# Attention scores of two heads issued in turn, into two banks that they share with the attention's outputs

## Chip, core and metric

One core of a Trainium2 chip runs the whole kernel. The metric is the time of one execution on the device in microseconds (us). TensorE multiplies matrices and writes to PSUM, which has eight banks; VectorE (DVE in the profile), ScalarE (ACT) and GpSimd (POOL) work on what lies in SBUF, the first two also on PSUM; DMAs are issued from SyncE (SP). Every engine works off its own queue in order, and waits at the head of the queue hold up all that stands behind.

## What is computed

```python
def _attn_ref(q, k, v, f_logit):                  # (4, 8, 768, 48) each
    f = 1.0 / (1.0 + np.exp(-f_logit))
    for t in range(S):
        state = f[:, :, t, :, None] * state + np.einsum('bhd,bhe->bhde', k[:, :, t], v[:, :, t])
        y[:, :, t] = np.einsum('bhd,bhde->bhe', q[:, :, t], state)

x = y as 3072 tokens x 384
x = (max(x @ w_in, 0) ** 2) @ w_out               # 384 -> 2048 -> 384
P = exp(logits of x @ w_gate), eight rounds of row and column normalisation
out = sum over 8 experts of P[:, e] * (max(x @ w1[e], 0) @ w2[e])   # 384 -> 1024 -> 384
```

All of it is in fp32 (the first mixture's weights reach the chip as 64-bit numbers). The state is decayed per channel, so that the attention is computed in chunks.

## The kernel before

**Attention.** The 3072 tokens are 24 chunks of 128, six for each of four sequences. Eight heads of 48 channels lie as four pairs: one head of a pair in partitions 0 to 47, the other in 64 to 111. For each chunk `c` the steps are: a sigmoid of the gates (L312), two scans on VectorE (L319, L325) that make running decays, products of keys and queries with them (L329, L332), the scores (L344), the causal mask on VectorE that also takes them out of PSUM (L349, one instruction for the four pairs of one head), a transpose of the keys (L354, L358), the chunk's contribution to the state (L366) and the state's update (L371, L336), the output (`mix`, L383 from scores and values, L386 from the state), and its way out of PSUM: a rounded part on ScalarE (L417) and the rest on VectorE (L415).

**Scores.** `scores(c, j)` issues the four products of head `j` of each pair, into one bank. For `j` = 0 and 1 these are two steps, `sc0` and `sc1`. From chunk 3 on both use the one buffer of the pool `ps_p`, so `sc1` waits for the mask of `sc0` (`cm0`), and `sc0` of the next chunk for `cm1`; the output `y` has a bank of its own (`ps_y`). In the first three chunks, when the accumulators of the first mixture are still free, `sc1` and every second output use the banks of those.

**First mixture.** Eight blocks of 384 tokens (three chunks each), sixteen steps a block: nine long products (L500) in three roundings, ReLU and square (L505, L508), a split into two roundings (L512 on ScalarE, L516 on VectorE), and nine long products (L526) into three banks of accumulators, two steps later. Block `j` needs the output of its three chunks, the first block that of chunks 0 to 2. Within the first block, step `f` also needs weight block `f`, which is converted from 64-bit numbers: two steps on ScalarE (L909, L912), three on VectorE (L916, L920, L924), a sum on GpSimd (L928), a rounding on ScalarE (L281) and the rest by L284 (on VectorE for ten of the sixteen, on GpSimd for six). The attention of the next block runs between the products of the current one.

**Second mixture.** It follows when the first is done (L679, L730, and VectorE, ScalarE and GpSimd around them); nothing of it is touched.

**What sets the order.** A planner (`Plan`) holds each step with its engine, a cost, a due time and the steps that it needs, and plays them forward; each engine's queue is in the order in which the planner starts the steps. Where TensorE would idle before the first products, it fills in small matmuls (`warm`, L246). So a changed cost, due time or need moves other steps too. Each fp32 product of scores or outputs is carried out as two passes, each with a load of weights and a matmul of its own in the profile; the long products (fp32r) are one pass.

Of the kernel before, what the change touches and what calls it, by code (L numbers as in the profile page):

```python
# [9 lines left out]
F32 = mybir.dt.float32  # L10
# [7 lines left out]
PSUM = bass.MemoryType.PSUM  # L18

B, H, S, DH = 4, 8, 768, 48  # L20
NP = H // 2
# [5 lines left out]
CH = 128  # L27
# [4 lines left out]
CPB = BT // CH  # L32
# [118 lines left out]
def body(tc, fkq, v, wm, wa, wc, gate, seqs, out):  # L151
# [37 lines left out]
    ps1 = ExitStack()  # L189
    ps_acc = ps1.enter_context(tc.tile_pool(name="ps_acc", bufs=1, space=PSUM))  # L190
    ps_p = ps1.enter_context(tc.tile_pool(name="ps_p", bufs=1, space=PSUM))
    ps_y = ps1.enter_context(tc.tile_pool(name="ps_y", bufs=1, space=PSUM))
# [8 lines left out]
    def if_(ok, name):  # L201
        return name if ok else None
# [33 lines left out]
    warm, acc1, tmp = {}, {}, {}  # L236
# [101 lines left out]
    def scores(c, j):  # L338
        kk = kq[c % 3]

        own = c >= CPB or j == 0
        tmp["p", j] = (ps_p if own else ps_acc).tile([128, NP, CH], F32, tag="pp" if own else "a1", name="pp")
        for p in range(NP):
            pe.matmul(tmp["p", j][:, p, :], kk[64 * j:64 * j + DH, 0, p, :], kk[64 * j:64 * j + DH, 1, p, :], start=True, stop=True)  # L344

    def causal(c, j):
        if j == 0:
            Psb[c] = ap2.tile([128, 2, NP, CH], F32, tag="Psb", name="Psb")
        dve.tensor_tensor(out=Psb[c][:, j], in0=tmp["p", j], in1=mask.to_broadcast([128, NP, CH]), op=ALU.mult)  # L349
# [25 lines left out]
    def new_y(c):  # L375
        own = c >= CPB or c % 2 == 0
        tmp["y", c] = (ps_y if own else ps_acc).tile([128, NP, CH], F32, tag="y" if own else "a2", name="y")
# [47 lines left out]
    for c in range(NCH):  # L425
# [5 lines left out]
        b2 = c >= 2  # L431
# [22 lines left out]
        at("sc0", "pe", 0.87, 0, lambda c: scores(c, 0), [("mulk", c), ("mulq", c), if_(c, ("cm0" if c < CPB else "cm1", c - 1))])  # L454
        at("cm0", "dve", 0.6, 0, lambda c: causal(c, 0), [("sc0", c), "masks", if_(b2, ("mix", c - 2))])
        at("sc1", "pe", 0.87, 1, lambda c: scores(c, 1), [("cm0", c)] if c >= CPB else [("sc0", c), if_(c, ("cm1", c - 1))])
        at("cm1", "dve", 0.6, 1, lambda c: causal(c, 1), [("sc1", c), ("cm0", c)])
# [9 lines left out]
        needs = [("cm0", c), ("cm1", c), ("ldv", c), if_(not first, ("sh", c)), if_(c > CPB, ("yl", c - 1)), if_(1 < c <= CPB, ("yl", c - 2 if c < CPB else c - 1))]  # L467
# [123 lines left out]
    def at(us):  # L591
        return n1 + us / 3.0
# [578 lines left out]
```

## Time and profile before

| | us |
|---|---|
| median of 3 runs (2186.46 to 2194.72) | 2186.51 |
| the profiled execution | 2187.32 |
| its span in the profile | 2185.5 |
| TensorE busy (97% of the span) | 2115.9 |
| VectorE busy (61%) | 1328.3 |
| chain that ended last: TensorE | 90% |
| of it L344, the scores | 2% |

The busy time of TensorE counts from the first of overlapping passes to the last. The share over the span is a mean over three stages with different limits: attention and weight conversion up to some 142 us, the first mixture with the rest of the attention up to 550 us, the second mixture after that. The granted clock of TensorE is at half in the first 19 us and full in most of the rest.

### The profile page before, as it was taken

The numbers are of one execution on the slowest core, as the hardware profiler recorded it, in microseconds if no ns is written. First come the engines' busy times: TensorE is split into PE (matmuls) and PEld (weight loads), VectorE is DVE, ScalarE is ACT, GpSimd is POOL, SyncE is SP. The second block draws the span as 40 slices with busy tenths as digits, with TensorE's granted clock in tenths as the row PEclk, the third lists the DMA queues.
The fourth block names the chain that finished last, engine by engine and source line by source line (L and its number), as shares of the span: only waits on it lengthen the run. The fifth ranks groups of instructions, "written<-read, shape, count | busy, mean of one in ns | idle before, by whom it ended". The sixth has DMA issues, their size and how long they took to land.

```text
span 2185.5 us, 27781 instructions
## 1 busy us (share of the span) xinstructions
PE 2115.9 (97%) x10668; PEld 1791.7 (82%) x10668; DVE 1328.3 (61%) x2016; ACT 885.5 (41%) x1505; POOL 648.9 (30%) x642
## 2 busy tenths in 40 slices
PE   8899999999986999999999999999999999999998
PEld 6789899998975888887887888888887888888886
DVE  7974433342365666765767766676668667666764
ACT  4654444443642333432433443344335334433441
POOL 4531100010010433343333333333333243334332
PEclk8899999999987999999999999999999999999999
DMA  6432211110111112111123211121123112111210
GB/s 248 138 115 62 86 57 63 63 56 12 60 55 39 63 55 68 55 64 46 54 68 110 68 54 54 58 68 53 54 68 111 61 54 64 54 61 61 68 44 31
DMA packets 55114, 148.76 MB, mean 68 GB/s; under 512 B 6332, under 2 KB 15548, under 8 KB 54972
## 3 DMA queue, kind: packets, MB, share of 16 engines
q1 hardware_dynamic: 54972, 146.90, 20.4%
q8 instruction: 85, 1.39, 0.3%
q14 instruction: 57, 0.47, 0.1%
HBM read 135.28 MB, written 9.54 MB: 66 GB/s over the span
## 4 chain that ended last, share of the span: by engine, by line
PE 90%; DVE 7%; issue 1%; DMA 1%; POOL 1%; ACT 0%; SPq 0%; POOLq 0%; DVEq 0%; ACTq 0%
PE o L730 34%; PE e L679 32%; PE e L500 9%; PE a L526 8%; PE pp L344 2%; PE y L383 1%; PE y L386 1%; PE lg L541 1%; DVE lo L516 1%; DVE cv_t L916 1%; DVE sg L319 1%; DVE cv_t L924 1%; DVE sg L325 1%; PE ds L366 1%; POOL acc L750 0%
## 5 line engine op out<-in xcount | busy, mean ns | idle before, releaser
L730 PE MATMUL o<-h,w 128*128 128x512 f32 x3456 | 794.4, 390 | 7.7 <-DVE acc L745 7.7
L730 PEld LDWEIGHTS o<-h,w 128*128 128x128 f32 x3456 | 649.5, 188 | 144.5 <-DVE acc L745 8.2
L679 PE MATMUL e<-x,w 128*128 128x512 f32 x3168 | 734.0, 392 | 9.6 <-DVE flag L887 4.5
L679 PEld LDWEIGHTS e<-x,w 128*128 128x128 f32 x3168 | 598.7, 189 | 136.4 <-ACT s L697 5.7
L750 POOL TENSOR_TENSOR acc<-acc,sc 128x512 f32<-128x512 f32 x270 | 349.9, 1303 | 574.7 <-DVE sc L745 566.8
L697 ACT COPY s<-e 128x512 f32<-128x512 f32 x288 | 169.2, 587 | 851.1 <-PE e L679 846.2
L745 DVE TENSOR_TENSOR sc<-o,pb 128x512 f32<-128x512 f32 x270 | 186.3, 690 | 384.9 <-PE o L730 339.5
L719 DVE SCALAR_TENSOR_TENSOR h<-v,h 128x512 fp32r<-128x512 f32 x384 | 277.8, 742 | 1.7 <-ACT h L714 1.3
L714 ACT ACTIVATE h<-v 128x512 fp32r<-128x512 f32 x384 | 242.5, 632 | 41.7 <-DVE v L706 41.6
L651 POOL TENSOR_TENSOR rawa<-rawa 128x256 f32<-128x256 f32 x96 | 84.2, 877 | 552.8 <-DMA rawa<-in_wa_dram 373.8
L706 DVE TENSOR_TENSOR v<-e,s 128x512 f32<-128x512 f32 x288 | 198.2, 688 | 75.5 <-ACT w L664 58.2
L500 PE MATMUL e<-x,w 128*128 128x384 f32 x1152 | 232.5, 346 | 7.6 <-DVE x L415 4.8
L516 DVE TENSOR_TENSOR lo<-g,hi 128x384 fp32r<-128x384 f32 x128 | 83.8, 655 | 234.0 <-ACT hi L512 234.0
L500 PEld LDWEIGHTS e<-x,w 128*128 128x128 f32 x1152 | 201.5, 191 | 16.6 <-DVE x L415 5.0
L526 PE MATMUL a<-hi,w 128*128 128x384 f32 x768 | 199.5, 341 | 0.0
L668 DVE TENSOR_TENSOR w<-rawa,w 128x768 fp32r<-128x768 f32 x192 | 158.1, 824 | 7.5 <-ACT w L664 7.5
L505 ACT ACTIVATE g<-e 128x384 f32<-128x384 f32 x128 | 62.9, 492 | 212.4 <-PE e L500 208.3
L664 ACT CAST w<-rawa 128x768 fp32r<-128x768 f32 x192 | 135.2, 729 | 27.5 <-POOL rawa L653 8.4
L526 PEld LDWEIGHTS a<-hi,w 128*128 128x128 f32 x768 | 140.8, 191 | 0.7 <-issue 0.4
L526 PE MATMUL a<-lo,w 128*128 128x384 f32 x384 | 131.0, 341 | 7.5 <-DVE lo L516 6.6
L329 POOL TENSOR_TENSOR kq<-kq,sg 128x512 f32<-128x512 f32 x24 | 31.8, 1323 | 316.6 <-DMA kq<-in_fkq_dram 167.9
L668 DVE TENSOR_TENSOR w<-rawc,w 128x768 fp32r<-128x768 f32 x96 | 91.6, 954 | 0.3 <-ACT w L664 0.2
(99 smaller groups left out, 1354.4 us busy)
## 6 DMA issues: line engine op xcount, KB each, us to landing
rawa<-in_wa_dram SPq DMA_DIRECT2D x96, 384.0 KB, 3.0
rawc<-in_wc_dram SPq DMA_DIRECT2D x96, 384.0 KB, 3.4
raw<-in_wm_dram SPq DMA_DIRECT2D x16, 768.0 KB, 5.8
pb<-ptd SPq DMA_DIRECT2D x24, 512.0 KB, 3.6
fraw<-in_fkq_dram SPq DMA_DIRECT2D x23, 512.0 KB, 3.8
kq<-in_fkq_dram SPq DMA_DIRECT2D x23, 512.0 KB, 4.9
vt<-in_v_dram SPq DMA_DIRECT2D x24, 192.0 KB, 5.0
x2d<-x2t SPq DMA_DIRECT2D x8, 576.0 KB, 2.8
```

The lines of the kernel that those rows point to most:

```text
L500: pe.matmul(ps, w[:, wl, k * 128:(k + 1) * 128], xx[:, xl, k, :], start=n == 0, stop=n == 3 * KD - 1)
L526: pe.matmul(acc1[j][m], w[:, wl, D + m * 128:D + (m + 1) * 128], g, start=f == 0 and n == 0, stop=f == NF - 1 and n == 2)
L664: act.copy(out=W2[g, k][:, 0, 0:n], in_=src)
L668: dve.tensor_tensor(out=W2[g, k][:, 1, 0:n], in0=src, in1=W2[g, k][:, 0, 0:n].bitcast(F32), op=ALU.subtract)
L679: pe.matmul(ps, w[a], x[b], start=start and n == 0, stop=stop and n == 2, skip_group_check=True)
L697: act.copy(out=snap[g, n], in_=bank[g, "a"])
L706: dve.tensor_tensor(out=vs[g, k], in0=bank[g, k], in1=other, op=ALU.add)
L714: act.activation(out=hs[g // 2, t, f][:, 0], in_=vs[g, k], func=ACTF.Relu)
L719: dve.scalar_tensor_tensor(out=h[:, 1], in0=vs[g, k], scalar=0.0, in1=h[:, 0].bitcast(F32), op0=ALU.max, op1=ALU.subtract)
L730: pe.matmul(ob[q, t, m], w[:, a, c:c + 128], h[:, b], start=f == 0 and n == 0, stop=f == 3 and n == 2)
L745: dve.tensor_tensor(out=dst, in0=ob[q, t, m], in1=pbt[p, e][:, t * TB:(t + 1) * TB], op=ALU.mult)
L750: pool.tensor_tensor(out=acc[p, t, m], in0=acc[p, t, m], in1=sc[q, t, m], op=ALU.add)
```

## The change

The scores of a chunk become one step, `sc`. It takes two buffers of `ps_p`, which now has two, and issues for each pair the product of head 0 and then that of head 1, each into its own bank. Both masks follow. The output of a chunk takes the next buffer of the same pool from chunk 3 on, so `sc` of the next chunk needs both masks (`cm1`) and, from chunk 4 on, the VectorE part of the previous output (`yl`, L415). In the first three chunks the outputs use two of the accumulators' banks in turn. `sc` is entered with a cost of 0.95 (two steps of 0.87 before), and `cm1` is due with `cm0`.

```diff
--- before.py
+++ after.py
@@ -188,8 +188,7 @@
     ap2 = left.enter_context(tc.tile_pool(name="ap2", bufs=2, reuse_waits="tile"))
     ps1 = ExitStack()
     ps_acc = ps1.enter_context(tc.tile_pool(name="ps_acc", bufs=1, space=PSUM))
-    ps_p = ps1.enter_context(tc.tile_pool(name="ps_p", bufs=1, space=PSUM))
-    ps_y = ps1.enter_context(tc.tile_pool(name="ps_y", bufs=1, space=PSUM))
+    ps_p = ps1.enter_context(tc.tile_pool(name="ps_p", bufs=2, space=PSUM))
 
     plan = Plan()
     add = plan.add
@@ -335,13 +334,14 @@
         Sh[c] = ap2.tile([128, NP, 64], F32, tag="Sh", name="Sh")
         dve.tensor_tensor(out=Sh[c], in0=Sst[c % 2], in1=sg[c % 2][:, 0, :, CH:CH + 1].to_broadcast([128, NP, 64]), op=ALU.mult)
 
-    def scores(c, j):
+    def scores(c):
+
         kk = kq[c % 3]
-
-        own = c >= CPB or j == 0
-        tmp["p", j] = (ps_p if own else ps_acc).tile([128, NP, CH], F32, tag="pp" if own else "a1", name="pp")
+        for j in range(2):
+            tmp["p", j] = ps_p.tile([128, NP, CH], F32, tag="pp", name="pp")
         for p in range(NP):
-            pe.matmul(tmp["p", j][:, p, :], kk[64 * j:64 * j + DH, 0, p, :], kk[64 * j:64 * j + DH, 1, p, :], start=True, stop=True)
+            for j in range(2):
+                pe.matmul(tmp["p", j][:, p, :], kk[64 * j:64 * j + DH, 0, p, :], kk[64 * j:64 * j + DH, 1, p, :], start=True, stop=True)
 
     def causal(c, j):
         if j == 0:
@@ -373,8 +373,8 @@
             dve.tensor_copy(out=t[:, :, 0:DH], in_=tmp["m"])
 
     def new_y(c):
-        own = c >= CPB or c % 2 == 0
-        tmp["y", c] = (ps_y if own else ps_acc).tile([128, NP, CH], F32, tag="y" if own else "a2", name="y")
+
+        tmp["y", c] = (ps_p if c >= CPB else ps_acc).tile([128, NP, CH], F32, tag="pp" if c >= CPB else f"a{1 + c % 2}", name="y")
 
     def mix_pair(c, p, rows=64):
         y, vv, kk, st = tmp["y", c], vt[c % 3], kq[c % 3], Sh.get(c)
@@ -451,10 +451,9 @@
             at("mulq", "dve", 0.65, -2, lambda c: mul_q(c, dve), [("scanf", c), ("ldk", c)])
         else:
             at("mulq", "pool", 1.25, -2, mul_q, [("scanf", c), ("ldk", c)])
-        at("sc0", "pe", 0.87, 0, lambda c: scores(c, 0), [("mulk", c), ("mulq", c), if_(c, ("cm0" if c < CPB else "cm1", c - 1))])
-        at("cm0", "dve", 0.6, 0, lambda c: causal(c, 0), [("sc0", c), "masks", if_(b2, ("mix", c - 2))])
-        at("sc1", "pe", 0.87, 1, lambda c: scores(c, 1), [("cm0", c)] if c >= CPB else [("sc0", c), if_(c, ("cm1", c - 1))])
-        at("cm1", "dve", 0.6, 1, lambda c: causal(c, 1), [("sc1", c), ("cm0", c)])
+        at("sc", "pe", 0.95, 0, scores, [("mulk", c), ("mulq", c), if_(c, ("cm1", c - 1)), if_(c > CPB, ("yl", c - 1))])
+        at("cm0", "dve", 0.6, 0, lambda c: causal(c, 0), [("sc", c), "masks", if_(b2, ("mix", c - 2))])
+        at("cm1", "dve", 0.6, 0.1, lambda c: causal(c, 1), [("sc", c), ("cm0", c)])
         misc = ("st", c - 1) if not first else (("st", c - 2) if c else None)
         lg = [("lgc", blk - 2)] if blk >= 2 and q == 0 else []
         if not last:
@@ -464,7 +463,7 @@
             at("st", "dve", 0.35, 2, state, [("ds", c), if_(not first, ("sh", c)), if_(c % NCB >= 2, ("sh", c - 1)), "pads"])
         if not first:
             at("sh", "dve", 0.35, 0, shat, [("st", c - 1), ("scanr", c), if_(c % NCB > 2, ("mix", c - 2))])
-        needs = [("cm0", c), ("cm1", c), ("ldv", c), if_(not first, ("sh", c)), if_(c > CPB, ("yl", c - 1)), if_(1 < c <= CPB, ("yl", c - 2 if c < CPB else c - 1))]
+        needs = [("cm0", c), ("cm1", c), ("ldv", c), if_(not first, ("sh", c)), if_(1 < c < CPB, ("yl", c - 2))]
         if blk:
             at("mix", "pe", 2.1 if not first else 1.1, 2.5, mix, needs)
         else:
```

The work on each engine stays the same, but for the number of filling matmuls (L246 before, L245 after). What the planner makes of it is shown at three places.

TensorE, chunk 13, in the stretch where TensorE is the bound: `pp` are the scores, `e` the first products (L500 before, L499 after), `a` the second ones (L526, L525), `ktr` the transposes. Before:

```order
L344 MATMUL pp<-kq_125 128x128 x4
L500 MATMUL e_2660<-x_2026,w 128x384 x9
L526 MATMUL a_2532<-hi,w 128x384 x2
L526 MATMUL a_2532<-lo,w 128x384
L526 MATMUL a_2533<-hi,w 128x384 x2
L526 MATMUL a_2533<-lo,w 128x384
L526 MATMUL a_2534<-hi,w 128x384 x2
L526 MATMUL a_2534<-lo,w 128x384
L354 MATMUL ktr<-shift,kq_125 128x128 x4
L344 MATMUL pp<-kq_125 128x128 x4
L500 MATMUL e_2703<-x_2026,w 128x384 x9
```

After:

```order
L344 MATMUL pp<-kq_122 128x128 x8
L499 MATMUL e_2664<-x_2012,w 128x384 x9
L525 MATMUL a_2538<-hi,w 128x384 x2
L525 MATMUL a_2538<-lo,w 128x384
L525 MATMUL a_2539<-hi,w 128x384 x2
L525 MATMUL a_2539<-lo,w 128x384
L525 MATMUL a_2540<-hi,w 128x384 x2
L525 MATMUL a_2540<-lo,w 128x384
L354 MATMUL ktr<-shift,kq_122 128x128 x4
L499 MATMUL e_2705<-x_2012,w 128x384 x9
```

The second block of four has gone from behind the transposes, and its products stand in the first block, which has eight.

VectorE, around the last weight conversion of the first block: `cv_t` and `w` are conversion steps, `sg` and `d` the scans, `Psb` the masks, `lo` the rest of the first mixture's hidden values. Before, from the third step on weight 15 to its last:

```order
L924 SCALAR_TENSOR_TENSOR cv_t<-raw_1035,cv_t 128x768
L516 TENSOR_TENSOR lo<-g,hi 128x384
L325 SCALAR_TENSOR_TENSOR sg_128<-sg_128,d_129 128x516
L326 TENSOR_TENSOR minf<-minf,sg_128 128x4
L349 TENSOR_TENSOR Psb<-pp,mask 128x512
L516 TENSOR_TENSOR lo<-g,hi 128x384
L317 MEMSET sg_127 128x8
L318 MEMSET d_129 128x4
L319 SCALAR_TENSOR_TENSOR sg_127<-sg_127,d_129 128x516
L320 TENSOR_SCALAR d_129<-sg_127 128x4
L321 RECIPROCAL d_129<-d_129 128x4
L284 TENSOR_TENSOR w<-cv_t,w 128x768
```

After, the same two ends:

```order
L923 SCALAR_TENSOR_TENSOR cv_t<-raw_1039,cv_t 128x768
L283 TENSOR_TENSOR w<-cv_t,w 128x768
L316 MEMSET sg_125 128x8
L317 MEMSET d_126 128x4
L318 SCALAR_TENSOR_TENSOR sg_125<-sg_125,d_126 128x516
L319 TENSOR_SCALAR d_126<-sg_125 128x4
L320 RECIPROCAL d_126<-d_126 128x4
L349 TENSOR_TENSOR Psb<-pp,mask 128x512
L283 TENSOR_TENSOR w<-cv_t,w 128x768
```

Before, the second scan of chunk 7 (L325), the first scan of chunk 8 (L319) and two `lo` stand between the two ends; after, it is the first scan of chunk 7 (L318) and the rest of weight 14 (L283). One mask stands there in both.

VectorE, ahead of the VectorE part of the output of chunk 2 (`x`), on which the first product of the first mixture waits. Before:

```order
L924 SCALAR_TENSOR_TENSOR cv_t<-raw_199,cv_t 128x768
L317 MEMSET sg_128 128x8
L318 MEMSET d_129 128x4
L319 SCALAR_TENSOR_TENSOR sg_128<-sg_128,d_129 128x516
L320 TENSOR_SCALAR d_129<-sg_128 128x4
L321 RECIPROCAL d_129<-d_129 128x4
L415 TENSOR_TENSOR x_280<-y,x_280 128x3x128
```

After:

```order
L919 TENSOR_SCALAR cv_t<-cv_t 128x768
L923 SCALAR_TENSOR_TENSOR cv_t<-raw_201,cv_t 128x768
L415 TENSOR_TENSOR x_269<-y,x_269 128x3x128
L316 MEMSET sg_125 128x8
L317 MEMSET d_126 128x4
L318 SCALAR_TENSOR_TENSOR sg_125<-sg_125,d_126 128x516
```

The scan of chunk 3 stood ahead of `x` and stands behind it now.

## Rows read from the trace of the kernel before

**Rows 1.** Stretches: length, busy us of PE, PEld, DVE, ACT, POOL; PEclk, DMA, GB/s.
```profile
28.00:142.30 114.30, 95.38 (x590) 79.62 (x590) 112.59 (x132) 67.47 (x105) 65.79 (x36) 0.88 0.45 152
142.30:550.00 407.70, 407.68 (x2859) 369.05 (x2860) 151.13 (x288) 181.71 (x344) 38.78 (x31) 1.00 0.17 57
```

**Rows 2.** TensorE in order of time: start, duration, instruction; the three waits.
```profile
44.52 5.62 PE L500 MATMUL e<-x,w 128*128 128x384 f32 x17 [4.79 <-DVE x L415]
...
130.92 2.00 PE L500 MATMUL e<-x,w 128*128 128x384 f32 x7 [2.43 <-DVE w L284]
...
142.32 3.91 PE L500 MATMUL e<-x,w 128*128 128x384 f32 x21 [0.40 <-DVE w L284]
```

**Rows 3.** TensorE in order of time, around both score blocks of chunk 13.
```profile
302.87 0.34 PE L526 MATMUL a<-lo,w 128*128 128x384 f32 x1
303.14 1.16 PE L344 MATMUL pp<-kq 48*128 48x128 f32 x8
304.23 1.83 PE L500 MATMUL e<-x,w 128*128 128x384 f32 x9
...
307.29 0.34 PE L526 MATMUL a<-lo,w 128*128 128x384 f32 x1
307.46 0.60 PE L354 MATMUL ktr<-shift,kq 128*128 128x128 f32 x4
307.99 1.16 PE L344 MATMUL pp<-kq 48*128 48x128 f32 x8
309.07 1.83 PE L500 MATMUL e<-x,w 128*128 128x384 f32 x9
```

**Rows 4.** The same view, transposes between long products.
```profile
507.73 0.60 PE L354 MATMUL ktr<-shift,kq 128*128 128x128 f32 x4
508.08 0.60 PE L526 MATMUL a<-hi,w 128*128 128x384 f32 x2
```

**Rows 5.** One line's instructions, 142 to 550 us: durations in ns, minimum, median, maximum.
```profile
L344 PEld LDWEIGHTS pp<-kq x272: 182/188/189, 161.9 to 537.7; 48*128 48x128 f32 x136
L344 PE MATMUL pp<-kq x272: 271/272/374, 161.9 to 537.9; 48*128 48x128 f32 x136
...
L386 PEld LDWEIGHTS y<-kq,Sh x240: 129/131/133, 172.0 to 547.1; 48*64 48x64 f32 x120
```

**Rows 6.** Weight loads, then passes, that overlap 113.285 to 113.30 us.
```profile
113.28 0.14 PEld L386 LDWEIGHTS y<-kq,Sh 48*64 48x64 f32 x2 [0.17 <-issue]
...
113.07 0.28 PE L383 MATMUL y<-Psb,vt 128*64 128x128 f32 x2
113.28 0.33 PE L386 MATMUL y<-kq,Sh 48*64 48x128 f32 x2
```

**Rows 7.** End of an output step, its L415, and the next scores.
```profile
315.44 0.43 PE L386 MATMUL y<-kq,Sh 48*64 48x128 f32 x4
...
316.67 0.66 DVE L415 TENSOR_TENSOR x<-y,x 128x512 fp32r<-128x512 f32 x1
...
319.13 1.16 PE L344 MATMUL pp<-kq 48*128 48x128 f32 x8
```

**Rows 8.** VectorE in order of time, ahead of its last weight conversion.
```profile
133.65 0.55 DVE L516 TENSOR_TENSOR lo<-g,hi 128x384 fp32r<-128x384 f32 x1
134.12 2.87 DVE L325 TENSOR_TENSOR_SCAN sg<-sg,d 128x516 f32<-128x516 f32 x1
...
137.57 1.16 DVE L516 TENSOR_TENSOR lo<-g,hi 128x384 fp32r<-128x384 f32 x1
138.69 0.07 DVE L317 MEMSET sg<- 128x8 f32 x1
...
140.38 1.89 DVE L284 TENSOR_TENSOR w<-cv_t,w 128x768 fp32r<-128x768 f32 x1
```

**Rows 9.** VectorE in order of time, ahead of L415 of chunk 2.
```profile
39.52 2.64 DVE L319 TENSOR_TENSOR_SCAN sg<-sg,d 128x516 f32<-128x516 f32 x1
...
43.94 0.53 DVE L415 TENSOR_TENSOR x<-y,x 128x384 fp32r<-128x384 f32 x1
```

## The prediction

> **What bounds the kernel now.** I read the busy times by stretch first, because the shares over the span mix three stages [rows 1]. From 28 to 142.3 us VectorE is busy 112.59 of 114.30 us and TensorE only 95.38: here the conversion of the sixteen first-layer weight blocks, done on VectorE between the scans and masks of the attention, sets the pace. From 142.3 to 550 us TensorE is busy 407.68 of 407.70 us: it never waits. After 550 us the second mixture runs, which the edit doesn't touch and which moves as a whole. Next the waits of TensorE in order of time [rows 2]. In the first 142 us it waits 4.79 us for the first block's x (L415) and 2.43 and 0.40 us for converted weights (L284); the last of these waits is at 142.32, inside the product that uses weight block 15. So the time is: when the last weight is converted, and then the sum of all TensorE work that stands behind it in the queue. A microsecond that TensorE saves behind 142.3 counts in full. One that it saves earlier only makes it wait longer for VectorE.
>
> **What a block of scores costs.** Today the four products of one head are one block; all lie in the same half of the array's rows and one bank. In fp32 each product is two passes, so a block is 8 rows. In the chunk shown [rows 3] the last product ahead of it starts at 302.87, the block at 303.14 and the product behind it at 304.23. That is 1.36 us from neighbour to neighbour, where two neighbours without a block between them stand 0.17 apart (307.29 to 307.46). A block thus costs 1.18 us (with the third decimal kept). Where the transposes (L354) stand right ahead of it, the two together take 307.29 to 309.07 = 1.78, less 0.17 = 1.61; transposes alone, beside long products, cost 0.35 [rows 4]; the block then costs 1.26. Inside a block one pass takes 272 ns from start to end [rows 5], and the block 1.16 us: the last pass starts 0.88 behind the first, the first is 0.10 longer than the rest (373 or 374), so passes follow each other every (0.88 - 0.10) / 7 = 0.112 us.
>
> Behind 142.3 us stand 34 such blocks (272 rows of 8 each [rows 5]), for 17 chunks: 25 at 1.18 and 9, behind transposes, at 1.26, together 40.8 us.
>
> **What the change makes of them.** Now the two heads alternate: 16 passes, one head in array rows 0 to 47 and the other in 64 to 111, each into its own bank. The trace of before has no block with that pattern, so I bound it. The nearest row is the last step of the attention, L386, whose two heads also alternate between array rows 0 to 47 and 64 to 111 (and, other than the scores, between column halves as well). There both heads' passes run at the same time [rows 6]: two loads of 0.13 us [rows 5] end within 0.14, two passes of 128 columns within 0.33, where in turn the second would end 0.112 later. If the scores do the same, eight pairs take what eight passes take now: a block of 16 passes costs 0.27 (into the block) + 0.88 + 0.01 (the pair's offset) + 0.20 (out of it) - 0.17 = 1.19 us. Then 17 x 1.19 = 20.2, and TensorE saves 40.8 - 20.2 = **20.6 us** behind the last weight. If the two halves take turns, the block is 0.27 + (0.10 + 15 x 0.112) + 0.20 - 0.17 = 2.08 us, 17 x 2.08 = 35.4, and only 5.4 us are saved, one way into and out of a block less for each chunk. I take the first end, because L386 is the one row with both array halves in turn.
>
> The Trainium skill, page "TensorEngine Tiling (Array Packing)", Key Properties, says that different tiles can load and multiply at the same time; that goes further than L386 shows, which has both row and column halves apart. The page "TensorE: Matmul & The Clock Gate" gives 3.07 times, not 4, for four row tiles (Measured speedup vs the span model). By that share of the ideal, as an estimate, a pair would take 0.112 / 0.77 = 0.146 us in place of 0.112, 7 x 0.034 x 17 = 4.0 us more in all; no run here shows it, and the sum below does not use it.
>
> **What moves across the last weight.** In TensorE's queue the product that waits for weight 15 has 15 second products (L526 groups) ahead of it before and 14 now, so one more stands behind it: nine passes at 0.17, +1.6 us. The numbers of transposes, state and output steps behind it are unchanged, and all 17 chunks of scores stay behind it.
>
> **When the last weight is converted.** VectorE has no slack there, so I count what stands ahead of the last L284 in its queue. One scan group less (L319 with its small neighbours: 138.69 to 140.38, 1.7 us), one second scan less (L325: 2.87 us at 134.12), one L516 less (0.55 to 1.16 us) [rows 8]; all other groups (48 conversion steps, 13 masks, 6 L415, 5 states) are as many as before. That is 5.1 to 5.7 us less work. Against it stands the start of the kernel, where VectorE now has both masks of a chunk in one go and may wait for TensorE where before it had a scan to do; the whole idle time between 28 and 142.3 is 1.7 us now and can grow. I take -4.5 us, with ends -8 and +1. In this stretch L415 of chunk 2 moves ahead of the scan of chunk 3 (39.52 to 43.94 [rows 9]), so the first long product should start 4 us earlier. That counts for nothing by itself, since the weights set the end of the stretch. TensorE can follow: it has 7 x 1.18 + 1.6 = 9.9 us less to do before weight 15, and was 0.4 us early there [rows 2].
>
> **The added wait.** The scores of a chunk now need the previous chunk's L415, because its output lies in one of the two banks. While they wait, the whole of TensorE's queue stands behind them. Cover: the output step ends at 315.44 + 0.43 = 315.87, L415 ends at 316.67 + 0.66 = 317.33, so 1.5 us later; the next scores start at 319.13 [rows 7], 3.3 us behind the output step, and the new order puts the state step or one more long product into that gap as well. So at least 1.8 us are to spare, and I cost the wait at nothing. The old wait of the second head for the first head's mask goes; it cost nothing behind 142.3 either.
>
> **The sum.** The profiled run took 2187.3 us for a span of 2185.5. 2187.3 - 20.6 + 1.6 - 4.5 = 2163.8. The median of the runs shown is 0.8 below the profiled one, so **2163 us**, -1.1%.
>
> **The rivals.**
> *Turns.* The two array halves take turns, because 128 columns of weights are loaded for each pass (a load every 0.11 us, as long as the pass) and the loads share a path. For: in a block of today loads and passes are equally close. Against: the paired loads of L386. Sum: -5.4 + 1.6, and -3 for the weights, since the three early blocks get no shorter: 2187.3 - 6.8 - 0.8 = 2179.7, so 2177 to 2182. The Trainium skill speaks for this one: the page "TensorE: Matmul & The Clock Gate" (Step-by-step: what each phase is for) has one read port for all weight loads; the paired loads of L386 show that this alone doesn't put them in a row.
>
> *Turns with a drain, slower than before.* Each change between array halves might cost what a change of tile form costs: from the last L383 pair at 113.07 to L386 at 113.28 it is 0.21, against 0.112 in step, 0.10 more [rows 6]. In 16 passes there are 7 changes (if a product keeps its two passes together) to 15. On top of the turns that is 17 x 0.7 = 12 to 17 x 1.5 = 25 us: 2192 to 2205. It decides against the change from about 0.03 us for each of 15 changes. Against: L386 changes halves inside a pair without any such gap.
>
> *The wait bites.* Overlap holds, but L415 is queued behind a scan and both masks of the next work on VectorE: 1.7 + 1.2 + 1.4 = 4.3 us against 1.8 to 2.3 to spare, so at most 2.5 us in each of the 11 chunks that follow another closely, 27 us; or VectorE loses its gain at the start. The queue has masks behind L415, not ahead, at most of these places, so some 8 us: 2171, within 2167 to 2180.
>
> **How the numbers follow.** Forecast 0.72, by itself 2158 to 2170 (weights -8 to +1, a pair up to 0.118 in place of 0.112, 0.8 us). Wait or lost weights 0.08, turns 0.14, drain 0.06. The range reaches over the turns: **2158 to 2182**; left out are the drain and the tails. A measurement of this kernel tells about 0.5% (11 us) from no change, so faster means under 2175.6 and slower over 2197.4: the forecast and most of the wait give 0.78 faster, the turns and the lower end of the drain 0.17 the same, the rest 0.05 slower.
>
> **What would show it.** In the changed kernel's profile a block of scores has 16 rows in about 1.17 us (right), in about 2.05 (turns), or more (drain). TensorE has no wait from the last L284 to the end of the attention; a wait of scores on L415 there would show the third rival. The last weight wait stands near 138 in place of 142.3, and the first L500 near 39 to 41 in place of 44.5. The stretch from the last weight wait to the end of the attention shortens by 19 us, and nothing changes after it. I am wrong if the block's 16 passes are not paired, or if the weights come later than 143.

## The result, and the profile after

| | before, us | after, us |
|---|---|---|
| median of the runs beside each other | 2186.57 | 2158.41 |
| the same comparison made again | 2185.74 | 2160.32 |
| the profiled execution (first comparison) | 2187.32 | 2158.78 |
| its span | 2185.5 | 2157.1 |
| TensorE busy | 2115.9 | 2083.4 |
| VectorE busy | 1328.3 | 1323.9 |

By the medians the change makes the kernel faster by 28.2 us in the first comparison and by 25.4 us in the second. The ratios of the two kernels, which are not quite the quotients of the medians, are 0.986 (95% interval 0.9836 to 0.9884) and 0.9881 (0.9865 to 0.9898). The forecast was 23.5 us less, 2163 us in a range from 2158 to 2182; the first median lies at the lower edge of that range, and one of its runs (2155.79) below it. The direction and the main term are right; one term is too small.

In the changed kernel the scores are L344 still, the first products L499, the second ones L525, the last step of a weight's conversion L283, `lo` L515 and the mask L349. First TensorE in order of time around chunk 13's scores, which answers to [rows 3]: start, duration, instruction.

```profile
305.83 1.16 PE L344 MATMUL pp<-kq 48*128 48x128 f32 x16
306.93 0.62 PE L525 MATMUL a<-hi,w 128*128 128x384 f32 x2
```

Sixteen passes now stand in 1.16 us, where [rows 3] has eight. The product ahead of them starts at 305.56, so from neighbour to neighbour it is 1.36 us, as for one old block. All 17 blocks behind the weights measure so; first to last start is 0.890 us in each.

The stretches of the profiled execution, which answer to [rows 1] (length, busy us of PE, PEld, DVE, ACT, POOL; PEclk, DMA, GB/s):

```profile
28.00:134.21 106.21, 83.59 (x559) 69.25 (x558) 104.05 (x121) 66.25 (x103) 58.09 (x32) 0.90 0.49 163
134.21:536.00 401.79, 401.49 (x2945) 368.57 (x2946) 156.42 (x301) 189.77 (x357) 43.88 (x36) 1.00 0.18 58
```

The picture is the one of before: VectorE full up to the last weight, TensorE full behind it. The boundary has moved from 142.3 to 134.2. The whole idle time of TensorE behind it is 0.30 us, one wait for `lo` at 141.02, and no wait of scores is left there.

The waits of TensorE that answer to [rows 2], and the one wait of scores on the output ahead of them (L415):

```profile
37.37 1.67 PE L499 MATMUL e<-x,w 128*128 128x384 f32 x8 [1.52 <-DVE d L317]
...
73.51 0.49 PE L344 MATMUL pp<-kq 48*128 48x128 f32 x2
74.51 1.16 PE L344 MATMUL pp<-kq 48*128 48x128 f32 x14 [0.52 <-DVE x L415]
...
82.60 1.65 PE L499 MATMUL e<-x,w 128*128 128x384 f32 x4 [4.45 <-DVE w L283]
...
129.27 1.49 PE L499 MATMUL e<-x,w 128*128 128x384 f32 x7 [0.79 <-DVE d L317]
131.85 0.61 PE L499 MATMUL e<-x,w 128*128 128x384 f32 x2 [1.09 <-ACT w L280]
134.21 3.04 PE L499 MATMUL e<-x,w 128*128 128x384 f32 x16 [1.74 <-DVE w L283]
```

The last weight wait comes 8.1 us earlier than in [rows 2]. Two of these rows are put down to a MEMSET on VectorE (`d`, L317) that follows the true releaser at once: at 37.37 that is `x` (L415), at 129.27 the last step of weight 14. The wait at 74.51 is the price of the shared banks; 8 us later TensorE waits 4.45 us for a weight, so nothing of it is paid.

Where the 28.5 us between the two profiled executions lie, by three places that are easy to find in both (the last weight wait; the first wait of the second mixture, at 636.19 before and 608.72 after; the end):

| stretch | before | after | less |
|---|---|---|---|
| start to the last weight wait | 142.32 | 134.21 | 8.1 |
| from there to the first wait of the second mixture | 493.9 | 474.5 | 19.4 |
| the rest, with what lies outside the span | 1551.1 | 1550.1 | 1.1 |

The second row was forecast at 19.0 and is right. The first was forecast at 4.5, so it is 3.6 us off. So the experiments ask two things: is it really the pairing of the array's halves that makes the 19.4, and where do the 3.6 us more at the start come from?

### The profile page after: what moved, and what is told of

The parts are those of the page before. It is cut to its first block, busy times and chain, and to the rows that moved or that the text cites. A ratio compares the mean times of both kernels' runs of the same rounds, so it can differ in the third digit from the quotient of the medians.

```text
span 2157.1 us, 27848 instructions
## 1 busy us (share of the span) xinstructions
PE 2083.4 (97%) x10686; PEld 1765.9 (82%) x10686; DVE 1323.9 (61%) x2016; ACT 886.1 (41%) x1505; POOL 646.8 (30%) x642
## 4 chain that ended last, share of the span: by engine, by line
PE 89%; DVE 6%; DMA 1%; issue 1%; POOL 1%; ACT 1%; SPq 0%; POOLq 0%; DVEq 0%; ACTq 0%
PE o L729 35%; PE e L678 33%; PE a L525 8%; PE e L499 8%; PE y L383 1%; PE y L386 1%; PE pp L344 1%; DVE cv_t L923 1%; PE lg L540 1%; DVE cv_t L915 1%; DVE lo L515 1%; DVE sg L318 1%; DVE cv_t L919 0%; POOL acc L749 0%; PE ds L366 0%
## 5 line engine op out<-in xcount | busy, mean ns | idle before, releaser
L499 PE MATMUL e<-x,w 128*128 128x384 f32 x1152 | 228.0, 341 | 10.9 <-DVE w L283 7.4
L499 PEld LDWEIGHTS e<-x,w 128*128 128x128 f32 x1152 | 199.8, 189 | 17.7 <-DVE w L283 8.8
L515 DVE TENSOR_TENSOR lo<-g,hi 128x384 fp32r<-128x384 f32 x128 | 85.0, 666 | 206.3 <-ACT hi L511 206.3
L525 PE MATMUL a<-hi,w 128*128 128x384 f32 x768 | 199.5, 341 | 0.0
L525 PE MATMUL a<-lo,w 128*128 128x384 f32 x384 | 131.0, 341 | 11.0 <-DVE lo L515 10.9
L525 PEld LDWEIGHTS a<-hi,w 128*128 128x128 f32 x768 | 139.9, 191 | 1.5 <-issue 0.3
```

The costliest lines, as they stand in the source:

```text
L499: pe.matmul(ps, w[:, wl, k * 128:(k + 1) * 128], xx[:, xl, k, :], start=n == 0, stop=n == 3 * KD - 1)
L525: pe.matmul(acc1[j][m], w[:, wl, D + m * 128:D + (m + 1) * 128], g, start=f == 0 and n == 0, stop=f == NF - 1 and n == 2)
```

## The experiments

**The heads in turn.** In the experiments "in turn" means the four products of head 0 and then the four of head 1, in place of the alternation that the change makes. The joint step and the two shared banks stay; only the order of the eight products changes. (Code is shortened where it has `...`.)

```diff
-        for p in range(NP):
-            for j in range(2):
-                pe.matmul(tmp["p", j][:, p, :], ...)
+        for j, p in [(j, p) for j in range(2) for p in range(NP)]:
+            pe.matmul(tmp["p", j][:, p, :], ...)
```

> The changed kernel with one edit: in the joint step of scores the four products of head 0 come first and then the four of head 1 (same banks, same waits, same order of all other work). Theory A, alternation lets the two array halves work at once: without it the 16 passes take 0.10 + 15 x 0.112 = 1.78 us from first to last start in place of 0.89, so 17 x 0.89 = 15 us more behind the last weight, and 0 to 2 us more ahead of it: 2173 to 2176 against 2158.8. Theory B, the gain came from one joint block with one way in and out and from the new order of the queues, or the chip pairs the halves anyway: within 3 us of the changed kernel.

Measured: 2173.59 us (2170.24 to 2179.07), ratio 0.9936 (0.9914 to 0.9958). TensorE around chunk 13's scores:

```profile
301.54 1.71 PE L343 MATMUL pp<-kq 48*128 48x128 f32 x16
303.18 1.15 PE L498 MATMUL e<-x,w 128*128 128x384 f32 x5
```

The block is 1.71 us long where the changed kernel has 1.16. From the last weight wait to the end the kernel takes 8.9 us more, and 17 x (1.71 - 1.16) is 9.4: so the alternation alone is worth about 9 us there. That is less than the 15 us of theory A; that the median falls into A's range is luck, since in the profiled execution another 7.8 us lie ahead of the weights (the last weight wait is at 142.05, with the clock at half from 8.4 to 29.0 us). Yet the block is shorter than sixteen passes in a row would be (0.10 + 15 x 0.112 = 1.78 from first to last start; measured 1.438). In the single records the second head's first pass starts at 509.30, while three passes of the first head are still to start (509.40 to 509.63). Some passes found a partner across the border of the two heads: without that, 17 blocks would be longer by another 17 x (1.78 - 1.44) = 5.8 us, an estimate from the same rows. So pairing is about 15 of the 19.4 us, and most of the rest is the one way in and out of a joint block, as the prediction had it for turns (5.4 - 1.6). How far past the border a pass can reach is what the next run asks.

**The heads by twos.** Two products of head 0, two of head 1, and again.

```diff
-        for p in range(NP):
-            for j in range(2):
+        for j, p in [(j, p) for h in range(2) for j in range(2) for p in (2 * h, 2 * h + 1)]:
```

> The heads alternate every two products (two of head 0, two of head 1, again) instead of every one. With the heads wholly in turn (the first experiment), eight passes of one head and then eight of the other took 1.438 us from first to last start, not the 1.78 of sixteen passes in a row: the first pass of the second head started while about three passes of the first head were still to come. Theory of a reach of some three passes: with four passes of a head in a row nearly every pass finds a partner, and a block takes 0.9 to 1.05 us from first to last start (0.890 in the changed kernel); behind the weights at most 17 x 0.15 = 2.6 us more than the changed kernel. Rival, only neighbours in the queue pair: 3 pairs at the changes of head and ten single passes, about 1.4 us and 17 x 0.5 = 9 us more behind the weights.

Measured: 2157.56 us in one run. The block:

```profile
304.46 1.26 PE L343 MATMUL pp<-kq 48*128 48x128 f32 x16
305.65 0.62 PE L524 MATMUL a<-hi,w 128*128 128x384 f32 x2
```

First to last start is 0.991 us in all 17, one step of 0.10 more than with strict alternation, and far from the 1.4 of the rival. The work of the other half needn't be the next instruction; with four passes in a row nearly all pair. (The single run's time is as low as the changed kernel's, though from the last weight wait to the first product of the second mixture it takes 2.1 us more, 455.5 against 453.4. Its last weight wait comes 2.2 us earlier, and its clock at the start was full; see the last section.)

**The first seven chunks in turn.** All that stands behind the weights is the changed kernel's; only the early blocks are long again.

```diff
-        for p in range(NP):
-            for j in range(2):
+        for j, p in [(j, p) for j in range(2) for p in range(NP)] if c < 7 else [(j, p) for p in range(NP) for j in range(2)]:
```

> The changed kernel; only chunks 0 to 6, whose scores stand ahead of the last converted weight, have their heads one after the other. Theory A, the conversions on VectorE set that stretch: the last weight wait stays at 134.2 within 1 us, and the time within 1 us of 2158.8. Theory B, the shorter early blocks are where the unforeseen 3.6 us ahead of the last weight came from: the wait moves back by 2 to 4 us, and so does the time, 2161 to 2163.

Measured: 2161.49 us (2159.94 to 2163.55), ratio 0.9872 (0.9832 to 0.9912). By the times alone that is hardly apart from the changed kernel; the trace is clearer, because both executions had the same clock in the first 28 us (0.88). VectorE's waits in order of time from 18 to 33 us, first of the kernel before, then of the changed one, then of this one:

```profile
19.88 0.69 DVE L349 TENSOR_TENSOR Psb<-pp,mask 128x512 f32<-128x512 f32 x1 [3.79 <-PE pp L344]
27.97 0.69 DVE L349 TENSOR_TENSOR Psb<-pp,mask 128x512 f32<-128x512 f32 x1 [0.78 <-PE pp L344]
```

```profile
19.39 0.69 DVE L349 TENSOR_TENSOR Psb<-pp,mask 128x512 f32<-128x512 f32 x1 [1.11 <-PE pp L344]
27.37 0.56 DVE L415 TENSOR_TENSOR x<-y,x 128x384 fp32r<-128x384 f32 x1 [1.02 <-ACT x L417]
29.94 0.35 DVE L371 TENSOR_TENSOR S<-Sh,ds 128x192 f32<-128x192 f32 x1 [0.72 <-PE ds L366]
```

```profile
21.07 0.69 DVE L348 TENSOR_TENSOR Psb<-pp,mask 128x512 f32<-128x512 f32 x1 [1.35 <-PE pp L343]
29.60 0.56 DVE L414 TENSOR_TENSOR x<-y,x 128x384 fp32r<-128x384 f32 x1 [1.57 <-ACT x L416]
32.72 0.35 DVE L370 TENSOR_TENSOR S<-Sh,ds 128x192 f32<-128x192 f32 x1 [1.26 <-PE ds L365]
```

VectorE, which sets the pace, waits for TensorE in the first 33 us: for scores, and for the output and the state that stand behind them. With the early blocks in turn each of these places comes 1.7 to 2.8 us later, the first long product at 40.15 in place of 37.37, and the last weight wait at 137.22 in place of 134.21. What is lost at the start is still there 100 us later, and 2.8 of the 3.0 us are there already at the first long product, so they are the loss of the first three blocks. (The first of them loses most: the clock is at half from 9.8 to 16.6 us in both executions, when the short block is nearly done and the long one has just begun, so it takes 3.06 us in place of 1.23.) Of these 3 us, 0.9 may be chance: the very first scores start at 9.75 in place of 8.88, ahead of anything that was edited, and the start of two kernels that are alike up to there differs by 1.5 us (first long product at 37.01 in the last experiment below, 38.55 in the one with two scans ahead). So the early blocks are worth 2 to 3 us, and theory B holds.

**The first three chunks in turn.** The same line with `c < 3`.

> The changed kernel, with the heads in turn in the scores of chunks 0 to 2 alone. With chunks 0 to 6 in turn all waits of TensorE from the first product of the first mixture on came 2.8 to 3.0 us later. Theory of the start: before the first mixture TensorE is on the path, and its first three score blocks carry that: 3 x 0.55 us at full clock, up to twice that at half clock, so the first long product and all behind it 1.6 to 3 us later, 2160 to 2161.5. Rival, chunks 3 to 6 carry it: the last weight wait stays at 134.2 and the time at 2158.4.

Measured: 2165.25 us (2162.25 to 2169.72), ratio 0.9881 (0.9826 to 0.9936). The last weight wait of the profiled execution is at 141.36. By itself this decides nothing, since the clock was at half from 8 to 28 us, so that two of the three blocks took 3.1 us each. But the run with all heads in turn had nearly the same clock there (0.65 against 0.64). Its first long product comes at 44.56, here at 44.54; its last weight wait at 142.05, here at 141.36. So chunks 3 to 6, in turn only there, cost 0.7 us, and the rival, that they carry the loss, falls. The size of the loss can't be read from this trace. Its lower two runs, 2162.25 and 2162.89, are 2 to 4.5 us above the changed kernel.

**The first product late.** Is it the first long product that carries the loss, or VectorE's queue ahead of it? Here TensorE alone is held up, and VectorE's order stays.

```diff
+        for _ in range(42 if i == 0 else 0):
+            pe.matmul(warm["t"], ident, ident, start=True, stop=True)
```

> The changed kernel, with 42 more filling matmuls on TensorE ahead of the very first product of the first mixture (42 x 0.107 = 4.5 us, of which 1.5 fill the wait there, so that product ends 2.7 to 3 us later). VectorE's order is as in the changed kernel. Theory A, VectorE is what passes a delay on: it has no wait for TensorE between 30 and 54 us, and TensorE waits 8.5 us for it at 54.4, so the last weight wait stays at 96.9 us behind where the first product stood (134.2 in a run with the same clock at the start) and the time at 2156 to 2159. Theory B, the first long product itself is on the path, since in four kernels of these experiments the last weight wait follows it by 96.8 to 97.1 us wherever it stands: last weight wait 2.7 us later, 2160.5 to 2161.5.

> The changed kernel once more, on the same chip as the experiment with the late first product, so that the two are read side by side: 2156 to 2159, with the last weight wait 96.9 us behind the first long series of products.

Measured: 2160.65 us (2157.1 to 2165.13) with the late product, 2160.32 (2157.25 to 2161.71) for the changed kernel beside it. TensorE of the late one:

```profile
36.55 9.54 PE L497 MATMUL warm<-shift 128*128 128x128 f32 x84
45.85 1.83 PE L501 MATMUL e<-x,w 128*128 128x384 f32 x9
...
56.79 0.44 PE L527 MATMUL a<-lo,w 128*128 128x384 f32 x1 [2.71 <-DVE lo L517]
...
136.62 1.65 PE L501 MATMUL e<-x,w 128*128 128x384 f32 x4 [1.74 <-DVE w L283]
```

The expectation counted 42 passes; each fp32 product is two, so it was 84 and 9.5 us. The test is the harder for it: the long series stands 8.4 us later (45.85 against 37.44 in the changed kernel beside it), but TensorE's wait for `lo` shrinks from 8.49 to 2.71 us. The last weight wait is 2.26 us later (136.62 against 134.36). Of that, 0.97 was there already at 30 us, ahead of the edit; the other 1.3 come by way of ScalarE, for which VectorE waits 2.70 us at 50.75. So a late first product costs 1.3 of 8.4 us. The times tell nothing: both kernels are within 0.4 us of each other, and the changed kernel itself is above the 2156 to 2159 that was expected. By the trace theory A holds in substance, though it expected none, and the fixed distance of 96.9 us between the two places, on which B rested, is an effect of VectorE's queue and no law.

**Two scans later, in the kernel before.** Two of VectorE's scans (the second of chunk 7 and the first of chunk 8) are kept behind the last weight conversion, as the change has them.

```diff
-        at("scanr", ..., [("sigr" if c < CPB else "sig", c), if_(c, ("scanf", c - 1)), "scan0"])
-        at("scanf", ..., [("scanr", c), ("sig", c)])
+        at("scanr", ..., [("sigr" if c < CPB else "sig", c), if_(c, ("scanf", c - 1)), "scan0", if_(c >= 8, ("cvl", NF - 1))])
+        at("scanf", ..., [("scanr", c), ("sig", c), if_(c >= 7, ("cvl", NF - 1))])
```

> The kernel before; only the planner's needs are extended so that the second scan of chunk 7 and the first of chunk 8 come behind the last weight conversion in VectorE's queue, as in the changed kernel. TensorE's queue is the same as before. Theory A, as in the prediction, VectorE's work ahead of the last L284 sets the stretch: the wait moves from 142.3 to about 137.7 (1.7 + 2.9 us less), the time to 2182.7. Theory B, TensorE itself is the bound from the wait for weight 14 (130.92) on, since it was only 0.40 us early for weight 15: the wait vanishes, and 0.4 us is all that is gained, 2186.9.

Measured: 2187.44 us (2184.71 to 2196.23), ratio 1.0005 (0.9985 to 1.0025). No gain. TensorE shows why, with VectorE's last step of weight 15 and the stretch between weights 14 and 15 (length, busy us, PEclk as the third number from the end):

```profile
141.33 1.50 PE L500 MATMUL e<-x,w 128*128 128x384 f32 x7 [2.27 <-DVE w L284]
142.76 2.07 PE L344 MATMUL pp<-kq 48*128 48x128 f32 x8
...
150.26 1.16 PE L344 MATMUL pp<-kq 48*128 48x128 f32 x8
151.35 4.95 PE L500 MATMUL e<-x,w 128*128 128x384 f32 x27
```

```profile
147.22 0.96 DVE L284 TENSOR_TENSOR w<-cv_t,w 128x768 fp32r<-128x768 f32 x1 [0.48 <-ACT w L281]
```

```profile
142.60:149.60 7.00, 7.00 (x25) 6.62 (x24) 6.19 (x11) 2.36 (x4) 2.82 (x4) 0.51 0.30 102
```

The wait for weight 15 is gone, but the product of weight 15 starts 10 us after that of weight 14 all the same: two score blocks and two second products stand between them. (All times of this execution are some 10 us late, since its clock was at half up to 54 us.) But TensorE is that slow there because its clock, behind the wait for weight 14, is at half for 7 us: the first score block takes 2.07 us, the second 1.16. The weight itself is ready at 148.18, 3.2 us before TensorE comes to it. At full clock that stretch would be 3.5 us shorter, an estimate from the row, and TensorE would come to weight 15 when it is ready. The kernel before has the same fall of the clock at the same place, from 131.8 to 138.6 us, and waited only 0.40 us for weight 15 [rows 2]. So there, with the clock at half, TensorE was as much the limit as VectorE, and theory B holds. What the scans would give with a full clock between weights 14 and 15, which the changed kernel has, this run doesn't show.

**The same two scans ahead again, in the changed kernel.**

```diff
-        add(("cvl", n), ..., [("cvh", n)])
+        add(("cvl", n), ..., [("cvh", n)] + ([("scanf", 7), ("scanr", 8)] if n == NF - 1 else []))
```

> The changed kernel, with the second scan of chunk 7 and the first scan of chunk 8 put back ahead of VectorE's last weight conversion (where the kernel before has them); one output step of TensorE moves between the products of weights 14 and 15 by that. Theory A, VectorE's queue sets the last weight also in the changed kernel: the last weight wait moves from 134.2 by 2.87 + 1.7 = 4.6 us, to about 138.8, and the time to 2162 to 2164. Theory B, TensorE itself sets the pace there, as it did when the same two scans were moved the other way in the kernel before: the wait grows, but less than 2 us of it reach the end, 2158 to 2160.5.

Measured: 2162.2 us (2159.79 to 2163.83), ratio 0.9866 (0.9813 to 0.9919). TensorE:

```profile
134.35 0.43 PE L383 MATMUL y<-Psb,vt 128*64 128x128 f32 x2 [2.30 <-DVE Psb L349]
...
140.62 2.71 PE L499 MATMUL e<-x,w 128*128 128x384 f32 x14 [0.92 <-DVE w L283]
```

The last weight wait is 6.3 us later than in the changed kernel's second execution (134.36). At the first long product it is 1.1 late already (38.55 against 37.44), so 5.2 are the scans' and what they moved, close to the 4.6 expected. But an output step of 2.9 us now stands ahead of that wait, so at the first product of the second mixture only 2.3 us are left (591.05 against 588.76), and 1.2 without the late start. The median, 2 to 4 us above the changed kernel's, looks like theory A; the trace is nearer to B. The scans cost 1 to 4 us, and the run leaves open how much.

**All scans from chunk 6 on later, in the changed kernel.** As the kernel-before variant above, with `c >= 6` in both lines.

> The changed kernel; only the planner's needs are extended so that all scans of chunks 6 and later come behind the last weight conversion, which takes about 7 us of VectorE's work from ahead of it and moves the scores of chunk 6 behind it. Theory A, VectorE sets the stretch: TensorE's waits of 1.2, 1.3, 0.8, 1.1 and 1.7 us between 119 and 134.2 shrink, the last weight wait ends 3 to 6 us earlier, and with 1.2 us of scores moved behind it the time is 2154 to 2157. Theory B, TensorE's own work sets it: within 1 us of 2158.8.

Measured: 2159.47 us (2158.2 to 2162.41), ratio 0.9866 (0.9826 to 0.9906). The time is that of the changed kernel. In the trace the weight-15 product comes 2.6 us earlier (131.57), though the first long product is 1.3 us later. Of what that gains, 1.2 us are paid behind the weight, where the scores of chunk 6 now stand, and up to 1.7 us go to the clock, which is at half there from 132.6 to 136.0 us. The first product of the second mixture starts at 587.29 us, in the two executions of the changed kernel at 587.62 and 588.76. So work that is put off past the last weight is paid behind it where it is TensorE's. Whether putting off scans alone gains a microsecond or two is less than these runs can tell.

**The output step in two halves.** [Rows 6] had shown that a change of tile form costs 0.10 us more than a step in form. The output step changes seven times in each chunk; here its four pairs from the scores come first, then the four from the state.

```diff
-        for p in range(NP):
-            mix_pair(c, p)
+        for p in range(NP):
+            for j in range(2):
+                pe.matmul(y[...], vv[...], Psb[c][:, j, p, :], start=p == 0, ...)
+        if st is not None:
+            for p in range(NP):
+                for j in range(2):
+                    pe.matmul(y[...], st[...], kk[...], start=False, ...)
```

> The changed kernel, with the output step written so that the four pairs from scores and values (L383) come first and the four pairs from the state (L386) behind them, instead of in turn. Each change of the tile's form costs about 0.10 us more than a step of the same form by the trace (0.21 against 0.11); six of eight changes of a chunk go, and 15 such output steps stand behind the last weight. Theory: TensorE saves 6 x 0.1 to 0.14 in each, 9 to 13 us in all, 2146 to 2150. Rival, the changes cost nothing, since the row halves run on their own: 2158.4.

Measured: 2146.67 us (2146.16 to 2147.09), ratio 0.9797 (0.9745 to 0.9849): 12 to 14 us below the changed kernel, and the fastest of all. An output step of the changed kernel, then of this one:

```profile
316.19 0.44 PE L383 MATMUL y<-Psb,vt 128*64 128x128 f32 x4
316.56 0.43 PE L386 MATMUL y<-kq,Sh 48*64 48x128 f32 x4
...
318.76 0.43 PE L386 MATMUL y<-kq,Sh 48*64 48x128 f32 x4
319.13 1.83 PE L499 MATMUL e<-x,w 128*128 128x384 f32 x9
```

```profile
311.50 1.09 PE L394 MATMUL y<-Psb,vt 128*64 128x128 f32 x16
312.52 1.09 PE L398 MATMUL y<-kq,Sh 48*64 48x128 f32 x16
313.54 1.83 PE L506 MATMUL e<-x,w 128*128 128x384 f32 x9
```

From the first pass to the next product it was 2.94 us and is 2.04: 0.15 us for each of the six changes, more than the 0.10 of [rows 6]. Fifteen such steps stand behind the last weight, 15 x 0.90 = 13.4 with the third decimal kept. From the last weight wait to the first product of the second mixture the kernel takes 441.0 us, the changed kernel's second execution 454.4 (588.76 - 134.36): 13.4 less. (In both of these the clock is at half for 3.4 us right behind the weights. In the first execution of the changed kernel it is not, and there it takes 453.4 us.)

## Where the prediction was right, and the step that failed

**What bounds the kernel: right.** Behind the last weight TensorE is busy 401.49 of 401.79 us, and what it saves there is saved in full. (Ahead of it the prediction names three waits of TensorE, 7.6 us together, of 18.9 us idle between 28 and 142.3 us [rows 1]. The others are waits for `lo` and for masks. The sum doesn't rest on them.)

**The score block: right to the hundredth.** Forecast 1.19 us, measured 1.36 - 0.17 = 1.19, and the stretch behind the weights shortens by 19.4 us against 20.6 - 1.6 = 19.0. The bound from L386 was the right one, although it was an inference from one row that differs in column halves too. Turns and turns with a drain are out: they needed a block of 2.05 us or more. Even with the heads wholly in turn the block is 1.71. Two halves side by side lose 0.01 us in a block (0.890 against 0.88 from first to last start). The Trainium skill, page "TensorE: Matmul & The Clock Gate" (Measured speedup vs the span model), gives 3.07 times in place of 4 for four row tiles; by that share the prediction estimated 4.0 us lost. For two halves this trace doesn't agree; four tiles were not run here.

**The added wait: right, with one place more.** Scores never wait for L415 behind the weights. They do once before, 0.52 us at 74.51 (1.29 us at 74.67 in the second execution), and nothing of it is passed on: the weight wait behind it ends 8.1 us later in both, at 82.60 and 82.77. "No wait from the last L284" is off by the 0.30 us for `lo`.

**When the last weight is converted: the step that failed.** The term was -4.5 us, with ends -8 and +1, and measured -8.1. It was worked out as 5.1 to 5.7 us less work in VectorE's queue, against which about 1 us was set for a worse start. VectorE's own rows divide what was measured. They show the time up to the last weight wait in the kernel before, in the changed one and in the one with seven chunks in turn (length, busy us of PE, PEld, DVE):

```profile
0.00:142.30 142.30, 119.22 (x744) 99.50 (x744) 130.08 (x168) 77.28 (x121) 72.94 (x54) 0.87 0.52 183
```

```profile
0.00:134.21 134.21, 107.56 (x753) 88.13 (x753) 123.51 (x160) 77.10 (x121) 67.46 (x50) 0.90 0.56 194
```

```profile
0.00:137.22 137.22, 111.02 (x754) 92.97 (x754) 123.60 (x160) 77.16 (x121) 67.27 (x50) 0.89 0.56 190
```

Its work is 6.6 us less (130.08 to 123.51), about 1 us more than forecast. Its idle time, the length less that, is 12.2, then 10.7 and 13.6 us: 1.5 us less where 1 us more was forecast. So some 2.5 of the 3.6 us are idle time, and the start did not get worse but better: in the first 28 us VectorE is idle 10.5 us before and 8.5 us after (28.00 less the 17.49 and 19.46 of the last section). With the same clock and the same work, the run with seven chunks in turn has nearly all of the 3.0 us of its later weight (2.9) as idle time of VectorE.

The view on which "VectorE has no slack" rested begins at 28 us [rows 1], and 10.5 of the 12.2 us idle lie ahead of that. There VectorE waits for TensorE: up to 33 us, 3.79 + 0.78 = 4.6 us in the kernel before, 1.11 + 1.02 + 0.72 = 2.9 in the changed one, and 1.35 + 1.57 + 1.26 = 4.2 when the early blocks are long again. The sentence that failed is "One that it saves earlier only makes it wait longer for VectorE". It is true of the first long product (8.4 us late cost 1.3), and so is "That counts for nothing by itself". It is false of the scores ahead of it, for which VectorE itself waits: with seven early blocks in turn, at the same granted clock, the last weight came 3.0 us later, of which 2 to 3 are theirs.

**What is not settled.** The kernel before was profiled with a slower clock in the first 28 us than the changed one (0.82 against 0.88). Half speed for 3.4 us more, (0.88 - 0.82) x 2 x 28, is up to 1.7 us of the 8.1, so the 1.5 us less of idle time between these two executions may be clock in part. The two comparisons of medians (28.2 and 25.4 us) leave the gain beyond the forecast between 2 and 5 us. Why VectorE's work shrank by 1 us more than the steps that were counted is not shown. What the scans are worth alone is open too: put off in the kernel before they gave nothing (ratio 1.0005), with TensorE at half clock as the limit, and put back in the changed one they cost 1 to 4 us.

## What to carry to other kernels

Where small fp32 products use half of the array's rows, issue those of the two halves mixed, into two banks: two blocks then take the time of one, and the passes needn't even alternate strictly. Beside that, group passes of one tile form: here six changes fewer in a step were worth as much as half of the whole change. And before writing that an early saving "is only waited away", look into the first microseconds as well: what matters is whether the engine that sets the pace itself waits for the saving engine anywhere. Its busy and idle time from the very start to the place where the next engine takes over show that at once.

## What the runs showed of the hardware

**The two row halves reach past each other.** With eight passes of one half and then eight of the other, first to last start is 1.438 us, not 1.78; by fours it is 0.991; in strict alternation 0.890. In the single records of the first of these, a pass of the idle half can start while some three passes of the busy half that stand ahead of it are still to start.

**The clock at the start is not the same in each execution.** The first 28 us of the kernel before, of the run by twos, of the changed kernel and of the run with three chunks in turn (length, busy us, PEclk as the third number from the end):

```profile
0.00:28.00 28.00, 23.84 (x155) 19.88 (x156) 17.49 (x37) 9.82 (x17) 7.15 (x18) 0.82 0.84 310
```

```profile
0.00:28.00 28.00, 23.86 (x226) 18.86 (x226) 21.01 (x43) 12.37 (x20) 9.41 (x19) 1.00 0.92 336
```

```profile
0.00:28.00 28.00, 23.97 (x195) 18.87 (x196) 19.46 (x40) 10.86 (x18) 9.37 (x19) 0.88 0.85 312
```

```profile
0.00:28.00 28.00, 22.94 (x134) 19.40 (x135) 15.29 (x34) 8.46 (x14) 6.40 (x18) 0.64 0.83 310
```

In the run by twos TensorE is at 2.4 GHz in all of these 28 us; in the last one it is at 1.2 GHz from 8 to 28 us, and has got through 134 passes in place of 226. In these three kernels, which differ little up to there, the last weight wait stands at 131.97, 134.21 and 141.36 us. The spread is larger than the effects looked for at the start, so a few microseconds there can be read only from executions with the same clock in these rows. What decides it wasn't tried. In the kernel before the clock is at half from 8.8 to 19.0 us, not in the whole of the first 19 us, and later too: from 43.0 to 49.8, 60.0 to 63.4, 77.0 to 87.4 and 131.8 to 138.6 us.
